# Prefills tied to work four units ahead, joined norm constants, merged output planes and column kinds in a residual block on one core

## The chip, the cores and the metric

The kernel runs on one core of one Trainium2 chip. The metric is the device time of one execution in microseconds (us), as the median of several runs. A ratio, with its 95% interval, is taken from the record: it compares one kernel's fast runs with the other kernel's fast runs of the same rounds on the same chip, so it is not quite the ratio of the medians quoted beside it.

TensorE is the matmul engine, VectorE and ScalarE work elementwise, GpSimd does small things and issues the accumulating output writes, SyncE issues most of the other transfers (DMAs). In the traces here the engines take their instructions in the order in which the built program lists them, and they wait on semaphores for each other.

## The reference, cut to what matters

```python
def reference(x, t_emb, g1, be1, w1, w_emb, g2, be2, w2):   # B=2, C=512, 64x64, bf16
    h = conv3(_silu(gn(x, g1, be1)), w1)                    # gn: 4 groups of 128 channels
    h = h + (_silu(t_emb) @ w_emb).reshape(B, C, 1, 1)
    h = conv3(_silu(gn(h, g2, be2)), w2)
    return x + h
```

## The kernel before

The two 3x3 convolutions are computed with fewer products than nine taps: VectorE forms sums and differences of rows and columns of the input (the products' inputs, per channel tile `ct`), TensorE multiplies them with transformed weights, ScalarE takes the results out of PSUM, and VectorE combines them into output planes. The work is cut into 8 chunks (layer, batch, half image) of 4 units (output channel tiles): 32 units. Units 0 to 15 are layer 1, units 16 to 31 layer 2.

The order of all instructions is not written by hand. The kernel first records about 2,800 operations with an assumed cost each, a small list scheduler in the kernel orders them, and they are then issued in that order. The scheduler knows the exact elements that an operation reads and writes. The semaphores are put in afterwards by the layer that records the program, which goes by the operands' access patterns.

The parts that the change touches:

```python
        # output planes of a unit: two instructions of 1024 elements
        tt(tw(SD, 512), M(0, 2), M(2, 2), AD, nm + "s")          # two sums into SD, SD+512
        tt(M(0, 2), M(2, 2), M(0, 2), SB_, nm + "d")             # two differences into MB
        scal(se[0], M(2), M(1), 8.0, nm + "8")
        scal(se[1], M(3), M(1), 2.0, nm + "2")
        scal(se[2], A(SD + 1024, [[1, 512]]), A(SD + 512, [[1, 512]]), 4.0, nm + "4")
        tt(yr(0), A(MB, [[0, 2], [1, 512]]), A(MB + 1024, [[512, 2], [1, 512]]), AD, nm + "y")
        tt(yr(16), A(SD, [[0, 2], [1, 512]]), A(SD + 1024, [[-512, 2], [1, 512]]), AD, nm + "y")

        # column kinds of one channel tile: four instructions
        for kind, (i, j, op) in enumerate(((32, 33, SB_), (1, 0, SB_), (33, 0, SB_), (33, 0, AD))):
            tt(A(vnest(c, ct, kind, 0), [[1, 256 * nf]]), X(i), X(j), op, nm)

    # norm constants of one channel tile: small matmuls into PSUM bank 7, a VectorE copy
    # out of it, five further small instructions, of which one on GpSimd (the -0.5 power)
    def gn_chain(layer, b, ct, mes, name, SB=7, slack=2.5): ...

                # x copied into the output in DRAM, which the result is later added to
                dma(out[b, k, ch][:, r0:r1], x[b, k, ch][:, RW + r0:RW + r1], [], [...],
                    P * YF, f"pre{c}{k}")
```

The last one is called a prefill below: 32 copies of 260 KB from DRAM to DRAM, which depend on nothing.

## Time and profile before

| | before |
|---|---|
| median | 527.14 us of 3 runs (524.67 to 527.91) |
| span of the profiled run | 523.0 us |
| TensorE / VectorE / ScalarE busy | 473.8 / 445.7 / 383.9 us |
| last matmul to the end | 14 us |

The view by stretches of time, kernel before. Columns: stretch in us, its length, busy time of TensorE (matmuls), its weight loads, VectorE, ScalarE, GpSimd, each with the number of instructions, then granted TensorE clock, share of the DMA engines, GB/s.

```profile
core 0: us, PE busy (x) PEld busy (x) DVE busy (x) ACT busy (x) POOL busy (x), PEclk, DMA share, GB/s
60.00:136.00 76.00, 53.20 (x223) 23.71 (x221) 56.22 (x124) 56.31 (x126) 1.46 (x2) 0.80 0.64 201
136.00:200.00 64.00, 61.58 (x348) 33.45 (x347) 58.46 (x151) 58.29 (x105) 1.47 (x2) 1.00 0.39 131
200.00:285.00 85.00, 79.40 (x446) 42.98 (x445) 79.72 (x178) 65.31 (x121) 7.99 (x15) 0.99 0.61 199
285.00:335.00 50.00, 50.00 (x315) 30.58 (x314) 48.55 (x102) 38.14 (x52) 2.90 (x7) 0.98 0.51 167
335.00:509.00 174.00, 174.00 (x1239) 119.82 (x1236) 154.61 (x257) 120.46 (x137) 21.04 (x25) 1.00 0.57 129
```

In the last two lines TensorE is busy for all of 50 and 174 us: layer 2, which begins at 310 us, has no hole. The holes are in the first line (76.00 - 53.20 = 22.8 us) and in the third.

From the list of waits, kernel before (who waited, for whom, us in total, times, longest):

```profile
PE psum L369 <- DVE ar L318: 21.8, 8, 6.7
...
PE psum L369 <- DVE fs L421: 8.1, 5, 5.3
```

L318 is the helper of all large VectorE additions, L421 the copy that empties bank 7 in a chain of norm constants. The longest of its waits in the timeline of the kernel before (start, length, what, in brackets the idle time before it and what ended it):

```profile
274.39 7.83 DVE L318 TENSOR_TENSOR ar<-ar 128x1024 f16<-128x1024 f16 x12
...
277.57 0.50 PE L369 MATMUL psum<-fs,ones_neg 128*128 128x2 f32 x4
277.93 1.03 PE L369 MATMUL psum<-ar 128*128 128x256 f16 x8
...
284.07 0.15 DVE L421 COPY fs<-psum 128x2 f32<-128x2 f32 x1
...
284.27 6.07 PE L369 MATMUL psum<-ar 128*128 128x512 f16 x29 [5.31 <-DVE fs L421]
```

TensorE put its four small matmuls into bank 7 at 277.57 us, and the copy that frees the bank stood in VectorE's order behind long additions until 284.07 us.

The two sizes of the large additions, from the groups by shape (busy us, mean ns of one, idle time before them), and the prefills (first and last start, us), kernel before:

```profile
L318 DVE TENSOR_TENSOR ar<-ar 128x1024 f16<-128x1024 f16 x272 | 180.4, 693 | 18.4 <-ACT ar L341 17.3
...
L318 DVE TENSOR_TENSOR ar<-ar 128x2048 f16<-128x2048 f16 x16 | 19.5, 1220 | 7.0 <-ACT ar L341 7.0
```

```profile
L354 SPq DMA_DIRECT2D out_dram<-in_x_dram x32: 511/532/647, 39.2 to 115.6; - x32
```

### The profile page before, as it was taken

The page shows a single profiled execution, that of the slowest core. Times are in us where ns is not written, and L with a number is a line of the kernel's source. Part 1 is how long each engine was busy: PE and PEld are TensorE (multiplying, and loading weights), DVE is VectorE, ACT ScalarE, POOL GpSimd, SP SyncE. Part 2 cuts the span into 40 slices and gives each one's busy share as a digit, 9 for nine tenths or more (in the row PEclk, how much of TensorE's full clock was granted, in tenths as well). Part 3 has the DMA queues.
Part 4 walks back from the last instruction along what each step waited for, and adds up shares of the span by engine and source line. Part 5 has one row for each costly group of instructions (what it writes and reads, how often), then busy time and mean ns, then how long its engine had stood idle before and what let it go on. Part 6 is the DMA issues. An engine that isn't in the chain of part 4 may idle for free.

```text
span 523.0 us, 8270 instructions
## 1 busy us (share of the span) xinstructions
PE 473.8 (91%) x2889; PEld 281.2 (54%) x2889; DVE 445.7 (85%) x932; ACT 383.9 (73%) x614; POOL 44.1 (8%) x75
## 2 busy tenths in 40 slices
PE   6999986664999999999995999999999999999990
PEld 5744332322545554555553557766666777766660
DVE  1799757588799999999999999999999999986443
ACT  4896838588999986686987678597866878665440
POOL 3100000000100001001100000120200111001000
PEclk9999989785999999999998999999999999999995
DMA  8938848674545236467575456663773776268422
GB/s 328 327 111 249 272 126 249 182 233 159 163 154 175 74 115 205 143 186 219 189 245 204 133 185 214 144 143 106 161 168 104 174 162 171 72 120 155 65 42 41
DMA packets 41065, 87.18 MB, mean 167 GB/s; under 512 B 6464, under 2 KB 16448, under 8 KB 41024
## 3 DMA queue, kind: packets, MB, share of 16 engines
q1 hardware_dynamic: 35808, 77.07, 45.0%
q0 software_dynamic: 4928, 9.59, 12.0%
q8 instruction: 22, 0.36, 0.3%
q14 instruction: 19, 0.16, 0.1%
q10 hardware_dynamic: 288, 0.01, 0.0%
HBM read 62.25 MB, written 31.85 MB: 180 GB/s over the span
## 4 chain that ended last, share of the span: by engine, by line
issue 21%; DVE 20%; PE 6%; POOL 2%; ACT 2%; POOLq 0%; DVEq 0%; ACTq 0%
DVE ar L318 19%; PE psum L369 6%; POOL out_dram L354 2%; ACT ar L341 2%; DVE ar L322 1%; POOLq L1121 0%; DVE fs L846 0%; DVE fs L422 0%; DVE fs L435 0%; POOL ar L358 0%; DVE fs L433 0%; DVE fs L421 0%; DVE fs L841 0%; POOLq L354 0%; DVE fs L425 0%
## 5 line engine op out<-in xcount | busy, mean ns | idle before, releaser
L369 PE MATMUL psum<-ar 128*128 128x256 f16 (+2 forms) x2737 | 456.1, 327 | 30.1 <-DVE ar L318 21.8
L318 DVE TENSOR_TENSOR ar<-ar 128x1040 f16<-128x1040 f16 (+6 forms) x681 | 412.2, 654 | 48.6 <-ACT ar L341 31.6
L369 PEld LDWEIGHTS <-ar 128*128 128x128 f16 (+1 forms) x2729 | 264.4, 98 | 216.0 <-issue 31.5
L341 ACT ACTIVATE ar<-ar 128x512 f16<-128x512 f16 (+7 forms) x206 | 169.7, 852 | 62.0 <-DVE ar L318 47.9
L341 ACT ACTIVATE ar<-psum 128x512 f16<-128x512 f32 (+2 forms) x221 | 154.7, 716 | 55.6 <-PE psum L369 29.8
L341 ACT ACTIVATE ar<-ar,fs 128x2112 f16<-128x2112 bf16 (+1 forms) x32 | 68.5, 2144 | 7.4 <-DMA ar<-h_scr 2.6
L354 POOL DMA_DIRECT2D out_dram<-ar x16 | 19.3, 1206 | 126.8 <-DVE ar L318 105.6
L322 DVE TENSOR_SCALAR ar<-ar 128x512 f16<-128x512 f16 (+2 forms) x72 | 26.0, 385 | 1.6 <-ACT ar L341 1.6
L428 POOL TENSOR_TENSOR fs<-fs 128x1 f32<-128x1 f32 x16 | 13.5, 847 | 159.2 <-DVE fs L425 158.9
L341 ACT ACTIVATION_READ_ACCUMULATOR ar<-psum 128x1 f32 x96 | 19.4, 202 | 0.0
L369 PE MATMUL psum<-ar,ones_bf 128*128 128x260 bf16 x64 | 10.1, 317 | 4.4 <-DMA ar<-in_x_dram 4.4
L358 POOL MEMSET ar<- 128x65 f16 (+4 forms) x27 | 4.6, 212 | 110.9 <-DVE ar L318 38.2
L369 PEld LDWEIGHTS psum<-fs,ones_neg 128*128 128x128 f32 x72 | 10.3, 206 | 2.5 <-DVE fs L958 1.6
L341 ACT ACTIVATION_READ_ACCUMULATOR ar<-ar 128x1 f32 x56 | 10.7, 191 | 0.0
L369 PE MATMUL psum<-fs,ones_neg 128*128 128x1 f32 (+1 forms) x72 | 10.0, 247 | 0.7 <-DVE fs L958 0.7
L369 PEld LDWEIGHTS <-ones_bf 128*128 128x128 bf16 x64 | 6.9, 112 | 6.2 <-issue 3.1
L354 POOL DMA_DIRECT2D ar<-ar x4 | 3.7, 922 | 73.6 <-ACT ar L341 52.2
L421 DVE COPY fs<-psum 128x2 f32<-128x2 f32 x16 | 2.5, 156 | 6.8 <-PE psum L369 6.8
L889 DVE SCALAR_TENSOR_TENSOR ar<-psum,ident 128x128 bf16<-128x128 f32 x4 | 1.2, 289 | 5.5 <-PE psum L369 5.5
L969 DVE BATCH_NORM_STATS2 fs<-ar 128x6 f32<-128x512 bf16 x8 | 5.4, 686 | 0.0
L433 DVE TENSOR_TENSOR fs<-fs 128x1 f32<-128x1 f32 x16 | 2.5, 155 | 2.4 <-POOL fs L428 2.4
L422 DVE SCALAR_TENSOR_TENSOR fs<-fs 128x1 f32<-128x1 f32 x16 | 3.4, 213 | 0.0
(43 smaller groups left out, 30.5 us busy)
## 6 DMA issues: line engine op xcount, KB each, us to landing
ar<-in_w_dram SPq DMA_DIRECT2D x32, 384.0 KB, 3.7
ar<-in_x_dram SPq DMA_DIRECT2D x16, 552.5 KB, 4.1
out_dram<-in_x_dram SPq DMA_DIRECT2D x32, 260.0 KB, 4.0
h_scr<-ar SPq DMA_DIRECT2D x16, 520.0 KB, 3.2
ar<-h_scr SPq DMA_DIRECT2D x16, 520.0 KB, 4.5
out_dram<-ar POOLq DMA_DIRECT2D x16, 520.0 KB, 6.0
u_scr<-ar SPq DMA_DIRECT2D x16, 384.0 KB, 2.9
ar<-u_scr SPq DMA_DIRECT2D x4, 1536.0 KB, 7.1
```

The source lines that it names most:

```text
L318: pl.op("DVE", 0.075 + 0.000521 * out.n, lambda: nc.vector.tensor_tensor(out=out.ap, in0=a.ap, in1=b.ap, op=op), regs(a, b), regs(out), name)
L322: pl.op("DVE", cost or 0.075 + 0.00026 * out.n, lambda: nc.vector.tensor_scalar(out=out.ap, in0=a.ap, scalar1=s, scalar2=None, op0=ALU.mul ...
L341: lambda: nc.scalar.activation(out=out.ap, in_=a.ap, func=func, scale=sc, **kw), regs(*rr), regs(*ww), name)
L354: lambda: eng.dma_start(out=out, in_=in_, **kw), regs(*r), regs(*w), name, lat=3.2 if sw else None)
L358: pl.op("POOL" if eng == "gpsimd" else "DVE", 0.08 + 0.0005 * out.n, lambda: e.memset(out.ap, v), (), regs(out), name)
L369: nc.tensor.matmul(out.ap, lhsT=lhsT.ap, rhs=rhs.ap, start=st, stop=sp, skip_group_check=True)
L421: pl.op("DVE", 0.16, lambda: nc.vector.tensor_copy(out=F(tot, 2).ap, in_=ps.ap), regs(ps), regs(F(tot, 2)), name)
L422: pl.op("DVE", 0.1, lambda: nc.vector.scalar_tensor_tensor(out=F(nv).ap, in0=F(tot).ap, scalar=F(tot).ap, in1=F(tot + 1).ap, op0=ALU.mult, ...
L428: pl.op("POOL", 0.25, lambda: nc.gpsimd.tensor_tensor(out=F(rs).ap, in0=F(nv).ap, in1=F(NEGH).ap, op=ALU.pow), regs(F(nv)), regs(F(rs)), name)
L433: pl.op("DVE", 0.1, lambda: nc.vector.tensor_mul(out=F(s).ap, in0=F(rs).ap, in1=F(g).ap), regs(F(rs)), regs(F(s)), name)
L889: pl.op("DVE", 0.3, lambda: nc.vector.scalar_tensor_tensor(out=j2.ap, in0=g.ap, scalar=1.0 / HW, in1=ident[:], op0=ALU.mult, op1=ALU.mult, ...
L969: pl.op("DVE", 0.61, lambda e=e, q=q: nc.vector.bn_stats(out=q.ap, in_=e.ap), regs(e), regs(q), nm)
```

## The change

The intent: take the prefills out of the crowded beginning; join the norm constants of four channel tiles into one chain (12 chains become 3; the four of layer 1's batch 0 stay); save 60 VectorE instructions by merging pairs (32 output planes, 28 column pairs); and bring the scheduler's costs closer to the trace. Since the scheduler sees other operations and other costs, the order of everything changes too.

The diff, cut to its core:

```diff
-    LAT = {..., "DMA": 2.1}
+    LAT = {..., "DMA": 2.4}          # DMA rate 0.31 -> 0.3; silu + 0.18; GpSimd power 0.25 -> 0.85
 # prefills
-                        P * YF, f"pre{c}{k}")
+                        P * YF * 1.4, f"pre{c}{k}", after=ufirst[max(ucnt[0] - CFG["pre"], 0)])   # pre: 4
 # column kinds 0 and 1 by one instruction
-            tt(A(s0, [[1, 256 * nf]]), X(i), X(j), op, nm)             # four of them
+        tt(A(s0[0], [[s0[1] - s0[0], 2], [1, 256 * nf]]), X2(32, 1), X2(33, 0), SB_, nm)
+        for kind, op in ((2, SB_), (3, AD)):
+            tt(A(s0[kind], [[1, 256 * nf]]), X(33), X(0), op, nm)
 # output planes by one instruction
-        tt(tw(SD, 512), M(0, 2), M(2, 2), AD, nm + "s")
+        tt(tw(SD, 1024), M(0, 2), M(2, 2), AD, nm + "s")
-        scal(se[2], A(SD + 1024, [[1, 512]]), A(SD + 512, [[1, 512]]), 4.0, nm + "4")
+        scal(se[2], A(SD + 512, [[1, 512]]), A(SD + 1024, [[1, 512]]), 4.0, nm + "4")
-        tt(yr(0), A(MB, [[0, 2], [1, 512]]), A(MB + 1024, [[512, 2], [1, 512]]), AD, nm + "y")
-        tt(yr(16), A(SD, [[0, 2], [1, 512]]), A(SD + 1024, [[-512, 2], [1, 512]]), AD, nm + "y")
+        pq = lambda a, b, st: A(a, [[b - a, 2], [st, 2], [1, 512]])
+        tt(A(ys, [[RW, 32], [33, 2], [1, 32]]), pq(MB, SD, 0), pq(MB + 1024, SD + 512, 512), AD, nm + "y")
 # norm constants: gn_chain(..., n=1) takes n tiles; layer 2 and batch 1 of layer 1 use n=4
-        later.append(lambda: gn_chain(0, 1, ct, [(me, 0, 2)], nm))
+        if ct == CT - 1:
+            later.append(lambda: gn_chain(0, 1, 0, [(ME1, 0, 2 * CT)], "st1", n=CT))
 ... (gn2 likewise, per batch and no longer per tile)
```

The merged plane: the one instruction that now makes the output planes of a unit. Their first half lies in `MB`, their second in `SD`, 29,748 elements lower in layer 1 and 27,316 in layer 2 (from the layout).

More of the change, by code (lines that the diff above doesn't have):

```diff
@@ L31 @@
     WIN = {"DMA": 0.6}
-    LAT = {"PE": 0.12, "DVE": 0.12, "ACT": 0.15, "POOL": 0.15, "DMA": 2.1}
+    LAT = {"PE": 0.12, "DVE": 0.12, "ACT": 0.15, "POOL": 0.15, "DMA": 2.4}
     def __init__(self):
@@ L45, in space, with op @@
         self._space(name, size)
-    def op(self, eng, cost, fn, r=(), w=(), name="", chain=False, lat=None, slack=0.0):
+    def op(self, eng, cost, fn, r=(), w=(), name="", chain=False, lat=None, slack=0.0, after=None):
         o = Op()
@@ L76, in op @@
             self.chain = o.i
+        if after is not None:
+            deps.add(after)
         deps.discard(-1)
@@ L198 @@
     'np': 1,
+    'pre': 4,
     'wpe': (1, 0, 0, 0),
@@ L254 @@
     ar = pool.tile([P, NA], F16, name="ar")
-    NF = 512
+    NF = 640
     fs = pool.tile([P, NF], F32, name="fs")
@@ L339, in act @@
             kw["saturate"] = False
-        pl.op("ACT", 0.1 + 0.000833 * out.n + (0.09 if acc is not None else 0.0),
+        pl.op("ACT", 0.1 + 0.000833 * out.n + (0.09 if acc is not None else 0.0) + (0.18 if bias is not None else 0.0),
               lambda: nc.scalar.activation(out=out.ap, in_=a.ap, func=func, scale=sc, **kw), regs(*rr), regs(*ww), name)
@@ L347, in scal, with dma @@
             ts(out, a, s, name)
-    def dma(out, in_, r, w, nbytes, name="", sw=False, acc=False):
-        rate = 0.15 if acc else 0.31
+    def dma(out, in_, r, w, nbytes, name="", sw=False, acc=False, after=None):
+        rate = 0.15 if acc else 0.3
         kw = {"accum_op": ALU.add, "max_dma_last_dim": 2080} if acc else {}
@@ L353, in dma @@
         pl.op("DMA", nbytes / rate * 1e-6 if nbytes > 30000 else 0.1,
-              lambda: eng.dma_start(out=out, in_=in_, **kw), regs(*r), regs(*w), name, lat=3.2 if sw else None)
+              lambda: eng.dma_start(out=out, in_=in_, **kw), regs(*r), regs(*w), name, lat=3.2 if sw else None, after=after)
     def memz(eng, out, name="", v=0.0):
@@ L386 @@
     WJ = Fc(12)
-    NEGH = Fc(1)
-    EPSC = Fc(1)
+    NEGH = Fc(CT)
+    EPSC = Fc(CT)
     def scol(layer, b, ct):
@@ L400 @@
     nc.scalar.activation(out=fs[:, WARM:WARM + 1], in_=fs[:, WARM + 1:WARM + 2], func=ACT.Silu)
-    nc.vector.memset(fs[:, NEGH:NEGH + 1], -0.5)
-    nc.vector.memset(fs[:, EPSC:EPSC + 1], EPS)
+    nc.vector.memset(fs[:, NEGH:NEGH + CT], -0.5)
+    nc.vector.memset(fs[:, EPSC:EPSC + CT], EPS)
     nc.gpsimd.tensor_tensor(out=fs[:, WARM:WARM + 1], in0=fs[:, WARM + 1:WARM + 2], in1=fs[:, NEGH:NEGH + 1], op=ALU.pow)
@@ L408, with Fs, small, gn_chain @@
     ssb = T(s_sb[:], "s_sb")
-    def gn_chain(layer, b, ct, mes, name, SB=7, slack=2.5):
-        ps = Ps(SB, 0, [[1, 2]])
+    def Fs(c, step, n):
+        return R(fs[:, c:c + (n - 1) * step + 1:step], ("F", np.arange(n) * step + c), n)
+    def small(fn, r, w, name, cost=0.125):
+        pl.op("DVE", cost, fn, regs(*r), regs(*w), name)
+    def gn_chain(layer, b, ct, mes, name, SB=7, slack=2.5, n=1):
+        V = nc.vector
+        ps = Ps(SB, 0, [[1, 2 * n]])
         lst = []
-        for i, (c, k0, n) in enumerate(mes):
-            lst.append((Ps(SB, k0, [[1, n]]), cneg, F(c, n), i == 0, False))
-        lst.append((Ps(SB, 1, [[1, 1]]), cneg, F(EPSC), False, True))
+        for i, (c, k0, m) in enumerate(mes):
+            lst.append((Ps(SB, k0, [[1, m]]), cneg, F(c, m), i == 0, False))
+        lst.append((Ps(SB, n, [[1, n]]), cneg, F(EPSC, n), False, True))
@@ L419, in gn_chain @@
         mm(lst, name, chain=False, slack=slack)
-        tot, nv, rs = Fc(2), Fc(1), Fc(1)
-        pl.op("DVE", 0.16, lambda: nc.vector.tensor_copy(out=F(tot, 2).ap, in_=ps.ap), regs(ps), regs(F(tot, 2)), name)
-        pl.op("DVE", 0.1, lambda: nc.vector.scalar_tensor_tensor(
-            out=F(nv).ap, in0=F(tot).ap, scalar=F(tot).ap, in1=F(tot + 1).ap, op0=ALU.mult, op1=ALU.add),
-            regs(F(tot, 2)), regs(F(nv)), name)
-        pl.op("DVE", 0.1, lambda: nc.vector.tensor_scalar(
-            out=F(nv).ap, in0=F(nv).ap, scalar1=-1.0, scalar2=EPS, op0=ALU.mult, op1=ALU.max),
-            regs(F(nv)), regs(F(nv)), name)
@@ L428, in gn_chain @@
-        pl.op("POOL", 0.25, lambda: nc.gpsimd.tensor_tensor(
-            out=F(rs).ap, in0=F(nv).ap, in1=F(NEGH).ap, op=ALU.pow),
-            regs(F(nv)), regs(F(rs)), name)
+        tot, nv, rs = Fc(2 * n), Fc(n), Fc(n)
         s, nb = scol(layer, b, ct), ncol(layer, b, ct)
         g = GB + 2 * CT * layer + ct
-        pl.op("DVE", 0.1, lambda: nc.vector.tensor_mul(out=F(s).ap, in0=F(rs).ap, in1=F(g).ap),
-              regs(F(rs)), regs(F(s)), name)
-        pl.op("DVE", 0.1, lambda: nc.vector.scalar_tensor_tensor(
-            out=F(nb).ap, in0=F(tot).ap, scalar=F(s).ap, in1=F(g + CT).ap, op0=ALU.mult, op1=ALU.add),
-            regs(F(tot, 2), F(s)), regs(F(nb)), name)
+        T0, T1, N, S, B = F(tot, n), F(tot + n, n), F(nv, n), F(s, n), F(nb, n)
@@ new lines, in gn_chain @@
+        pl.op("DVE", 0.16, lambda: V.tensor_copy(out=F(tot, 2 * n).ap, in_=ps.ap), regs(ps), regs(F(tot, 2 * n)), name)
+        if n == 1:
+            small(lambda: V.scalar_tensor_tensor(
+                out=N.ap, in0=T0.ap, scalar=T0.ap, in1=T1.ap, op0=ALU.mult, op1=ALU.add), [T0, T1], [N], name, 0.2)
+        else:
+            small(lambda: V.tensor_mul(out=N.ap, in0=T0.ap, in1=T0.ap), [T0], [N], name)
+            small(lambda: V.tensor_add(out=N.ap, in0=N.ap, in1=T1.ap), [N, T1], [N], name)
@@ new lines, in gn_chain @@
+        small(lambda: V.tensor_scalar(out=N.ap, in0=N.ap, scalar1=-1.0, scalar2=EPS, op0=ALU.mult, op1=ALU.max),
+              [N], [N], name)
+        pl.op("POOL", 0.85, lambda: nc.gpsimd.tensor_tensor(
+            out=F(rs, n).ap, in0=N.ap, in1=F(NEGH, n).ap, op=ALU.pow), regs(N), regs(F(rs, n)), name)
+        small(lambda: V.tensor_mul(out=S.ap, in0=F(rs, n).ap, in1=F(g, n).ap), [F(rs, n)], [S], name)
+        if n == 1:
+            small(lambda: V.scalar_tensor_tensor(
+                out=B.ap, in0=T0.ap, scalar=S.ap, in1=F(g + CT).ap, op0=ALU.mult, op1=ALU.add), [T0, S], [B], name, 0.2)
+        else:
+            small(lambda: V.tensor_mul(out=B.ap, in0=T0.ap, in1=S.ap), [T0, S], [B], name)
+            small(lambda: V.tensor_add(out=B.ap, in0=B.ap, in1=F(g + CT, n).ap), [B], [B], name)
@@ L638, in rows_b @@
         X = lambda i: A(xb + i, [[RW, 8 * nf], [1, 32]])
-        for kind, (i, j, op) in enumerate(((32, 33, SB_), (1, 0, SB_), (33, 0, SB_), (33, 0, AD))):
-            s0 = vnest(c, ct, kind, 0)
-            tt(A(s0, [[1, 256 * nf]]), X(i), X(j), op, nm)
+        X2 = lambda i, j: A(xb + i, [[j - i, 2], [RW, 8 * nf], [1, 32]])
+        s0 = [vnest(c, ct, kind, 0) for kind in range(4)]
+        tt(A(s0[0], [[s0[1] - s0[0], 2], [1, 256 * nf]]), X2(32, 1), X2(33, 0), SB_, nm)
+        for kind, op in ((2, SB_), (3, AD)):
+            tt(A(s0[kind], [[1, 256 * nf]]), X(33), X(0), op, nm)
     ucnt = [0]
+    ufirst = {}
     prs = [0]
@@ L692, in unit @@
         nm = f"u{c}{k}"
+        if opening != 1:
+            ufirst[u] = len(pl.ops)
         last = u == 31
@@ L701, in unit @@
             OO = [O0[u % 3] + PL, O0[u % 3]]
-        if l == 0 and ch == 0 and (b, k) not in SSUM:
-            SSUM[(b, k)] = (Fc(12), Fc(2))
+        if l == 0 and ch == 0 and b not in SSUM:
+            SSUM[b] = (Fc(48), Fc(2 * CT))
         acc = lambda i: None
         if l == 0:
-            cs, cq = SSUM[(b, k)]
-            acc = lambda i: F(cs + 6 * ch + i)
+            cs, cq = SSUM[b]
+            acc = lambda i: F(cs + 12 * k + 6 * ch + i)
         fid = ACT.Identity if l == 0 else ACT.Copy
@@ L801, in unit @@
         scal(se[1], M(3), M(1), 2.0, nm + "2")
-        scal(se[2], A(SD + 1024, [[1, 512]]), A(SD + 512, [[1, 512]]), 4.0, nm + "4")
-        yr = lambda r0: A(ys + r0 * RW, [[RW, 16], [33, 2], [1, 32]])
-        tt(yr(0), A(MB, [[0, 2], [1, 512]]), A(MB + 1024, [[512, 2], [1, 512]]), AD, nm + "y")
-        tt(yr(16), A(SD, [[0, 2], [1, 512]]), A(SD + 1024, [[-512, 2], [1, 512]]), AD, nm + "y")
+        scal(se[2], A(SD + 512, [[1, 512]]), A(SD + 1024, [[1, 512]]), 4.0, nm + "4")
+        pq = lambda a, b, st: A(a, [[b - a, 2], [st, 2], [1, 512]])
+        tt(A(ys, [[RW, 32], [33, 2], [1, 32]]), pq(MB, SD, 0), pq(MB + 1024, SD + 512, 512), AD, nm + "y")
         yo = A(ys, [[24 * RW, 2], [1, PL]])
@@ L815, in unit @@
             dma(h_scr[b, k, ch], yv.ap, [yv], [K("h", b, k, ch)], P * YF * 2, nm + "st")
-            act(A8(JNK, YF), yv, ACT.Square, scale=float(HW) ** -0.5, acc=F(cq + ch), name=nm + "sq")
-            if ch == 1:
-                later.append(lambda: gn2(b, k))
+            act(A8(JNK, YF), yv, ACT.Square, scale=float(HW) ** -0.5, acc=F(cq + ch * CT + k), name=nm + "sq")
+            if ch == 1 and k == CT - 1:
+                later.append(lambda: gn2(b))
         else:
@@ L823 @@
     later = []
-    def gn2(b, k):
-        cs, cq = SSUM[(b, k)]
-        m0, me, wj, ws = Fc(2), Fc(2), WJ, Fc(1)
-        nm = f"gn2_{b}{k}"
-        E = EMB + k * BB + b
-        V = nc.vector
-        pl.op("DVE", 0.12, lambda: V.scalar_tensor_tensor(
-            out=F(wj, 12).ap, in0=F(cs, 12).ap, scalar=1.0, in1=F(SUMW, 12).ap, op0=ALU.mult, op1=ALU.mult,
-            accum_out=F(m0).ap), regs(F(cs, 12)), regs(F(wj, 12), F(m0)), nm)
-        pl.op("DVE", 0.1, lambda: V.reduce_sum(out=F(m0 + 1).ap, in_=F(cq, 2).ap, axis=AX.X),
-              regs(F(cq, 2)), regs(F(m0 + 1)), nm)
-        pl.op("DVE", 0.1, lambda: V.scalar_tensor_tensor(
-            out=F(me).ap, in0=F(m0).ap, scalar=1.0 / HW, in1=F(E).ap, op0=ALU.mult, op1=ALU.add),
-            regs(F(m0), F(E)), regs(F(me)), nm)
-        pl.op("DVE", 0.1, lambda: V.scalar_tensor_tensor(
-            out=F(ws).ap, in0=F(m0).ap, scalar=1.0 / HW, in1=F(me).ap, op0=ALU.mult, op1=ALU.add),
-            regs(F(m0), F(me)), regs(F(ws)), nm)
-        pl.op("DVE", 0.1, lambda: V.scalar_tensor_tensor(
-            out=F(me + 1).ap, in0=F(ws).ap, scalar=F(E).ap, in1=F(m0 + 1).ap, op0=ALU.mult, op1=ALU.add),
-            regs(F(ws), F(E), F(m0 + 1)), regs(F(me + 1)), nm)
-        gn_chain(1, b, k, [(me, 0, 2)], nm)
-        nb, s = ncol(1, b, k), scol(1, b, k)
-        pl.op("DVE", 0.1, lambda: V.scalar_tensor_tensor(
-            out=F(nb).ap, in0=F(E).ap, scalar=F(s).ap, in1=F(nb).ap, op0=ALU.mult, op1=ALU.add),
-            regs(F(E), F(s), F(nb)), regs(F(nb)), nm)
@@ new lines, in gn2 @@
+    def gn2(b):
+        cs, cq = SSUM[b]
+        V = nc.vector
+        nm = f"gn2_{b}"
+        wj, m0, me, ws, t = Fc(48), Fc(CT), Fc(2 * CT), Fc(CT), Fc(CT)
+        E = Fs(EMB + b, BB, CT)
+        C = F(cs, 48)
+        M0, ME, MQ, W, Tt = F(m0, CT), F(me, CT), F(me + CT, CT), F(ws, CT), F(t, CT)
+        wt = fs[:, SUMW:SUMW + 12].unsqueeze(1).to_broadcast([P, CT, 12])
+        g3 = lambda c: fs[:, c:c + 48].rearrange("p (k s) -> p k s", s=12)
+        small(lambda: V.tensor_tensor(out=g3(wj), in0=g3(cs), in1=wt, op=ALU.mult), [C], [F(wj, 48)], nm)
+        small(lambda: V.reduce_sum(out=M0.ap, in_=g3(wj), axis=AX.X), [F(wj, 48)], [M0], nm)
+        small(lambda: V.tensor_add(out=MQ.ap, in0=F(cq, CT).ap, in1=F(cq + CT, CT).ap), [F(cq, 2 * CT)], [MQ], nm)
+        small(lambda: V.scalar_tensor_tensor(
+            out=ME.ap, in0=M0.ap, scalar=1.0 / HW, in1=E.ap, op0=ALU.mult, op1=ALU.add), [M0, E], [ME], nm)
+        small(lambda: V.scalar_tensor_tensor(
+            out=W.ap, in0=M0.ap, scalar=1.0 / HW, in1=ME.ap, op0=ALU.mult, op1=ALU.add), [M0, ME], [W], nm)
+        small(lambda: V.tensor_mul(out=W.ap, in0=W.ap, in1=E.ap), [W, E], [W], nm)
+        small(lambda: V.tensor_add(out=MQ.ap, in0=MQ.ap, in1=W.ap), [MQ, W], [MQ], nm)
+        gn_chain(1, b, 0, [(me, 0, 2 * CT)], nm, n=CT)
+        S, B = F(scol(1, b, 0), CT), F(ncol(1, b, 0), CT)
+        small(lambda: V.tensor_mul(out=Tt.ap, in0=E.ap, in1=S.ap), [E, S], [Tt], nm)
+        small(lambda: V.tensor_add(out=B.ap, in0=B.ap, in1=Tt.ap), [B, Tt], [B], nm)
@@ L939 @@
     prs[0] = 2
-    S1 = {}
+    ME1 = Fc(2 * CT)
     def stats1(ct):
         nm = f"st1{ct}"
-        me = Fc(2)
+        me, mq = ME1 + ct, ME1 + CT + ct
         if CFG["st1"][ct]:
@@ L957, in stats1 @@
                 accum_out=F(me).ap), regs(F(part, 6)), regs(F(wj, 6), F(me)), nm)
-            pl.op("DVE", 0.1, lambda: nc.vector.reduce_sum(out=F(me + 1).ap, in_=F(part + 6, 6).ap, axis=AX.X),
-                  regs(F(part + 6, 6)), regs(F(me + 1)), nm)
+            pl.op("DVE", 0.1, lambda: nc.vector.reduce_sum(out=F(mq).ap, in_=F(part + 6, 6).ap, axis=AX.X),
+                  regs(F(part + 6, 6)), regs(F(mq)), nm)
         else:
@@ L973, in stats1 @@
             pl.op("DVE", 0.1, lambda: nc.vector.scalar_tensor_tensor(
-                out=F(me + 1).ap, in0=F(mv).ap, scalar=F(mv).ap, in1=F(mv + 1).ap, op0=ALU.mult, op1=ALU.add),
-                regs(F(mv, 2)), regs(F(me + 1)), nm)
-        later.append(lambda: gn_chain(0, 1, ct, [(me, 0, 2)], nm))
+                out=F(mq).ap, in0=F(mv).ap, scalar=F(mv).ap, in1=F(mv + 1).ap, op0=ALU.mult, op1=ALU.add),
+                regs(F(mv, 2)), regs(F(mq)), nm)
+        if ct == CT - 1:
+            later.append(lambda: gn_chain(0, 1, 0, [(ME1, 0, 2 * CT)], "st1", n=CT))
     def emb():
```

## The prediction

> **What bounds it.** The profile's span is 523.0 us; TensorE is busy 473.8 us (91%), VectorE 445.7, ScalarE 383.9 (busy table). By stretches of time: from about 311 to 509 us TensorE is busy all the time, and output units leave every 12.36 us at the end (28672 columns, 2.3 per ns): only fewer columns would shorten that. TensorE's idle time lies elsewhere: about 23 us between 60 and 136 us (53.2 of 76 us busy, granted clock 0.80), 5.3 us at 279 us, some 3 us in 136-200, 14 us after its last matmul.
>
> In 60-136 TensorE waits for VectorE, which makes the next transformed weights; there VectorE itself waits 11 us for weight and input loads. All 32 prefills (input copied to the output in DRAM, 260 KB each) are issued from 39 to 116 us: half of the bytes then, and 0.5 us of queue time each. Small weight loads land in 3.2 us (median) then, 2.2 us in 120-200.
>
> The wait at 279 us is TensorE before bank 7, which a norm-constant chain holds until VectorE copies it (released by the copy at L421); the copy stood behind 12 long VectorE instructions. All such waits: 8.1 us, 5 times.
>
> **What changes.**
> 1. Prefills move to about 265-460 us, two per 12 us unit. Weight loads gain about 1 us each in each of about six double-buffered rounds, plus queue delays: -4 to -10 us in 60-136. In layer 2 DMA share rises from 0.57 to about 0.7; TensorE should stay full.
> 2. Norm chains: 12 (layer 2, and batch 1 of layer 1) become 3. Nine groups of 4 small fp32 matmuls go, 0.36 us each: -3 us, of which 2 in full stretches. Fewer holds of bank 7: -5 us. VectorE loses 6-7 us of small instructions.
> 3. 32 output pairs and 28 column pairs each become one instruction. The durations 693 ns (1024 elements) and 1220 ns (2048) give 0.51 ns per element plus 166 ns, of which some 90 overlap the neighbour: 0.08 us saved each, 4.6 us of VectorE in all. The Trainium skill, "VectorE: DVE Perf Modes" (perf-mode tier table), gives tensor_tensor 1224 ns for 2048 bf16 at double rate; the trace agrees with 1220, so I expect the merged forms to keep this rate. Mostly TensorE is full there, so it buys nothing. In the last unit the merged plane must wait for ScalarE's scaling: +0.2 us.
> 4. Costs in the scheduler (DMA, silu, pow) come nearer to the trace; the order changes: +-4 us.
>
> Sum: -8 (60-136), -5 (bank 7), -2 (matmuls), +1 to 2 for new small waits: -14 us on the clock, so 514 us.
>
> **What would show it.** No DRAM-to-DRAM copy before about 240 us; small weight loads there land in about 2.3 us; TensorE idle in 60-136 falls from 23 to about 14 us; waits on the bank-7 copy under 3 us; VectorE busy about 435 us; matmuls 2853 instead of 2889; unit period in layer 2 still 12.4 us, last matmul about 14 us before the end.
>
> **What would make it wrong.** The loop of 60-136 may be bound by VectorE, ScalarE and buffers, not DMA latency: then about -7 us remain. Joining batch 1's constants makes its first silu wait for all four tiles and may leave a hole near 145 us. The reshuffled order may put another long run before a copy that TensorE needs. Prefills beside the weight stream could starve layer 2.
>
> Faster by over 2%: 0.6; within 2%: 0.36; slower: 0.04. Range 503 to 524 us.

## More of the kernel before

All operands lie in one large array `ar` in SBUF, at offsets that the kernel lays out by hand:

```python
    AB = [o, o + AF]          # input tiles (loads, silu in place)
    o += 2 * AF
    YS = [o, o + YF]          # output planes of a unit, two buffers
    o += 2 * YF
    MB = o                    # four taken-out products of a unit, 4 x 512
    o += 4 * MS
    ...
    SD0 = Z + 10016           # sums of a unit, in layer 1
    SD1 = Z + 12448           # sums of a unit, in layer 2; Z lies far below AB
```

## The result, and the profile after

| | before | after |
|---|---|---|
| median | 526.2 us of 4 runs | 533.84 us of 4 runs (533.33 to 534.28) |
| ratio | | 1.0147, 95% interval 1.0121 to 1.0172 |
| span of the profiled run | 523.0 us | 532.0 us |
| TensorE / VectorE / ScalarE busy | 473.8 / 445.7 / 383.9 us | 471.6 / 439.4 / 383.7 us |
| matmul instructions | 2889 | 2853 |

The kernel became 1.5% slower. It does less work on TensorE and on VectorE, as intended, and takes longer, so the time went into waits.

The stretches, kernel after, same columns as before:

```profile
60.00:136.00 76.00, 59.44 (x256) 26.48 (x254) 56.63 (x108) 58.58 (x132) 0.00 (x0) 0.87 0.40 123
136.00:200.00 64.00, 52.26 (x281) 28.08 (x282) 56.80 (x117) 56.94 (x100) 1.45 (x1) 0.89 0.45 150
200.00:285.00 85.00, 82.77 (x460) 44.27 (x459) 75.43 (x143) 63.02 (x116) 6.23 (x12) 1.00 0.56 180
285.00:335.00 50.00, 44.78 (x267) 26.43 (x265) 49.71 (x89) 39.66 (x58) 0.59 (x5) 0.97 0.70 243
335.00:509.00 174.00, 169.37 (x1206) 116.71 (x1205) 149.38 (x215) 116.31 (x134) 20.07 (x23) 1.00 0.63 156
```

TensorE's idle time in 60-136 us fell from 22.8 to 16.6 us, but in the next stretch it rose from 2.4 to 11.7 us, and the stretches of layer 2, full before, now have holes (5.2 us in 285-335 and 4.6 us in 335-509). From the list of waits, kernel after:

```profile
PE psum L372 <- DVE ar L321: 17.4, 5, 6.7
PE psum L372 <- ACT ar L344: 9.6, 4, 4.0
PE psum L372 <- DVE fs L975: 9.4, 1, 9.4
PE psum L372 <- DVE fs L434: 5.0, 3, 2.5
```

The line of 9.6 us for ScalarE is new, all of it in layer 2 but 1 us. L975 with 9.4 us is the last step of batch 1's statistics; in the kernel before that step, L958 there, held TensorE once, for 0.7 us. The prefills did move, and the merged shape keeps its rate (kernel after, same views as before):

```profile
L357 SPq DMA_DIRECT2D out_dram<-in_x_dram x32: 517/588/1219, 258.0 to 451.3; - x32
```

```profile
L321 DVE TENSOR_TENSOR ar<-ar 128x1024 f16<-128x1024 f16 x188 | 127.7, 693 | 19.5 <-ACT ar L344 18.1
L321 DVE TENSOR_TENSOR ar<-ar 128x2048 f16<-128x2048 f16 x64 | 79.2, 1238 | 27.8 <-ACT ar L344 16.2 <-issue 4.5 <-DMA ar<-in_x_dram 4.2
```

The second line holds a clue, read to its end: the 64 instructions of 2048 elements have VectorE idle before them for 27.8 us, where the 16 of the kernel before had 7.0.

To see where the time went, I counted matmul columns in each trace (both hold all 999,424 columns of the convolutions) and noted when each unit's share had begun, in us from the first such matmul. This is an evaluation of the trace, not a view of the profile. `f_split2`, `near` and `near_late` are experiments of below.

| start of unit | before | after | f_split2 | near | near_late |
|---|---|---|---|---|---|
| 5 | 119.51 | 108.08 | 103.49 | 107.48 | 104.62 |
| 6 | 135.38 | 137.23 | 133.62 | 136.26 | 118.92 |
| 9 | 181.09 | 181.92 | 177.90 | 180.66 | 183.21 |
| 14 | 253.49 | 255.28 | 250.28 | 252.85 | 259.40 |
| 15 | 274.84 | 270.70 | 264.57 | 267.15 | 273.69 |
| 18 | 315.11 | 317.44 | 306.90 | 308.61 | 314.60 |
| 24 | 389.43 | 391.76 | 381.22 | 382.93 | 388.92 |
| 27 | 426.58 | 433.98 | 418.62 | 420.08 | 426.26 |
| end | 488.51 | 495.93 | 480.55 | 482.02 | 488.19 |

The kernel after is 11.4 us ahead at unit 5 and 1.8 us behind at unit 6. It gains 5.9 us at unit 14, where the wait of 5.3 us for bank 7 stood, and loses 6.5 us from unit 15 to 18 and 5.1 us from unit 24 to 27. Two questions follow: what are the losses in layer 2 and at the layers' boundary, and why did 11 us vanish between units 5 and 6?

### The profile page after: what moved, and what is told of

The parts are those of the page before. It is cut to its first block, busy times and chain, and to the rows that moved or that the text cites. A ratio compares the mean times of both kernels' runs of the same rounds, so it can differ in the third digit from the quotient of the medians.

```text
span 532.0 us, 8068 instructions
## 1 busy us (share of the span) xinstructions
PE 471.6 (89%) x2853; PEld 278.0 (52%) x2853; DVE 439.4 (83%) x795; ACT 383.7 (72%) x614; POOL 38.7 (7%) x66
## 5 line engine op out<-in xcount | busy, mean ns | idle before, releaser
L321 DVE TENSOR_TENSOR ar<-ar 128x1024 f16<-128x1024 f16 (+5 forms) x621 | 408.2, 703 | 68.0 <-ACT ar L344 40.4
L344 ACT ACTIVATE ar<-ar 128x384 bf16<-128x384 bf16 (+7 forms) x206 | 170.1, 856 | 66.6 <-DVE ar L321 59.2
L344 ACT ACTIVATE ar<-psum 128x512 f16<-128x512 f32 (+3 forms) x221 | 155.1, 716 | 52.7 <-PE psum L372 25.2
L344 ACT ACTIVATE ar<-ar,fs 128x2112 f16<-128x2112 bf16 (+1 forms) x32 | 68.5, 2143 | 14.3 <-DMA ar<-h_scr 4.4
L443 POOL TENSOR_TENSOR fs<-fs 128x1 f32<-128x1 f32 (+1 forms) x7 | 8.0, 1137 | 143.5 <-DVE fs L441 143.5
L372 PE MATMUL psum<-fs,ones_neg 128*128 128x1 f32 (+3 forms) x36 | 5.2, 258 | 9.5 <-DVE fs L975 9.4
L372 PE MATMUL psum<-ar,ones_bf 128*128 128x260 bf16 x64 | 8.9, 293 | 4.5 <-DMA ar<-in_x_dram 4.5
L372 PEld LDWEIGHTS psum<-fs,ones_neg 128*128 128x128 f32 x36 | 5.0, 205 | 10.6 <-DVE fs L975 9.7
L434 DVE COPY fs<-psum 128x2 f32<-128x2 f32 (+1 forms) x7 | 1.1, 159 | 4.5 <-PE psum L372 4.5
L372 PEld LDWEIGHTS psum<-ar 2*128 2x128 f32 x8 | 1.8, 323 | 5.7 <-DVE ar L321 5.7
L372 PE MATMUL psum<-ar,s_sb 128*2 128x512 bf16 x9 | 3.1, 458 | 0.0
(49 smaller groups left out, 21.4 us busy)
```

The lines of the kernel that those rows point to most:

```text
L321: pl.op("DVE", 0.075 + 0.000521 * out.n, lambda: nc.vector.tensor_tensor(out=out.ap, in0=a.ap, in1=b.ap, op=op), regs(a, b), regs(out), name)
L344: lambda: nc.scalar.activation(out=out.ap, in_=a.ap, func=func, scale=sc, **kw), regs(*rr), regs(*ww), name)
L372: nc.tensor.matmul(out.ap, lhsT=lhsT.ap, rhs=rhs.ap, start=st, stop=sp, skip_group_check=True)
L434: pl.op("DVE", 0.16, lambda: V.tensor_copy(out=F(tot, 2 * n).ap, in_=ps.ap), regs(ps), regs(F(tot, 2 * n)), name)
L443: pl.op("POOL", 0.85, lambda: nc.gpsimd.tensor_tensor(out=F(rs, n).ap, in0=N.ap, in1=F(NEGH, n).ap, op=ALU.pow), regs(N), regs(F(rs, n)), ...
```

## The experiments

Each kernel was checked for correct output; all are correct but two, which are told as such. Those made from the kernel after start from it and change only what is said. Eighteen runs gave a result. Four kernels had to be submitted a second time, since no chip ran them the first time; hence the 2 in some labels.

### First round: undo one part of the change at a time

Parts undone: the joined chain of batch 1 (a_st1_apart), the tie of the prefills (a_pre_free), the merged pairs (a_pairs_apart). And the joined chain of batch 1 moved one unit later in the program (a_st1_late).

```diff
 # a_st1_apart
-        if ct == CT - 1:
-            later.append(lambda: gn_chain(0, 1, 0, [(ME1, 0, 2 * CT)], "st1", n=CT))
+        later.append(lambda: gn_chain(0, 1, ct, [(me, 0, 2)], nm))
 # a_st1_late
+            if c == 1 and k == 1:
+                gn_chain(0, 1, 0, [(ME1, 0, 2 * CT)], "st1", n=CT)
+                prod(2, 0)                         # no longer after unit (1, 0)
 # a_pre_free
-                        P * YF * 1.4, f"pre{c}{k}", after=ufirst[...])
+                        P * YF, f"pre{c}{k}")
 # a_pairs_apart: two instructions per output plane and per column pair, as in the kernel before
```

> The kernel after, but the norm constants of batch 1 in layer 1 again as four chains, one per channel tile, each at its old place. Theory W (TensorE had run ahead; the stretch up to 147 us is set by the statistics work of VectorE, ScalarE and the DMA queue, whose last part ends near 143 us in both kernels): the wait before the last chain stays, 7 to 12 us near 130-147, and the time is within 3 us of the kernel after (533.8). Theory J (joining four chains into one made the wait of 9.4 us): the wait falls under 2 us and the time falls by 7 to 11 us, to 523-527.

> The kernel after, with the joined chain of batch 1 and the first product that needs it one unit later in program order, so that unit 5's bank-7 matmuls need not wait for it. Theory B (order in PSUM bank 7 holds TensorE): the 9.4 + 2.5 us wait vanishes and the time falls by 8 to 12 us, to 522-526. Theory W (work of the other engines bounds this stretch): the wait at 134 us vanishes but TensorE waits as much later, at the start of chunk 2 (about 190-200 us) for the products there; time within 4 us of 533.8.

> The kernel after, with the prefills untied again and at their old cost, so the scheduler puts them early. If the tie gave back TensorE time between 60 and 136 us (as the prediction said): TensorE idle there rises from 16.6 us to about 23 us. If that gain was spent again in the wait near 140 us (theory W): column progress at unit 6 is within 3 us of the kernel after, and the total within 4 us; if prefills beside layer 2's streams cost the 5 us lost after unit 24, the total falls by about 5 us.

> The kernel after, with the output planes and the two column kinds by two VectorE instructions each, as before. If merging costs layer 2 its 5 us (a plane waits for all three scalings): holes after unit 24 vanish and the time falls by 3 to 6 us. If merging is harmless: VectorE is about 4.6 us busier, and the time is within 4 us of 533.8, moved only by the new order.

| run | median us | ratio to before, 95% |
|---|---|---|
| a_st1_apart | 543.89 | 1.0317 to 1.0373 |
| a_st1_late | 536.96 | 1.0186 to 1.0239 |
| a_pre_free | 538.94 | 1.0216 to 1.0270 |
| a_pairs_apart | 518.29 | 0.9829 to 0.9887 |

Three of the four expectations missed. Only a_st1_late came out as one of its theories (W) had said: the wait near 134 us is gone, TensorE waits as much and more in 170-215 us (19.9 us in three waits for VectorE), and the time is 3.1 us longer. a_st1_apart took longer than both of its theories allow, and its 10 us of loss are not explained here. In a_pre_free, TensorE's idle time in 60-136 us was to rise to about 23 us and is 17.6 us; this returns below. Undoing the merges is worth 15 us, far more than the 3 to 6 us of the theory that blamed them; the other three made the kernel slower. But each of these kernels was scheduled anew, so its whole order differs. The next round keeps the order.

### Second round: the same order, other instructions

In f_split2 the scheduler sees the kernel after, so the order is the same to the last instruction, but where a merged instruction would be issued, two are issued, one after the other. In f_merge2 and b_merge2 the scheduler sees pairs (as a_pairs_apart and as before do), and the merged instruction is issued at the place of the second half. a_nudge2 changes one assumed cost by 0.2% and nothing else.

```diff
 # f_split2, at the place of the merged instruction
-            nc.vector.tensor_tensor(out=full[0].ap, in0=full[1].ap, in1=full[2].ap, op=op)
+            for o, (a, b) in zip(outs, ins):
+                nc.vector.tensor_tensor(out=o.ap, in0=a.ap, in1=b.ap, op=op)
 # a_nudge2
-        pl.op("DVE", 0.075 + 0.000521 * out.n, lambda: nc.vector.tensor_tensor(
+        pl.op("DVE", 0.075 + 0.000520 * out.n, lambda: nc.vector.tensor_tensor(
```

> The kernel after with its instruction order kept exactly, but each merged output plane and column pair issued as two VectorE instructions, back to back in the same place. Theory I (the merged instructions themselves cost: a plane that waits for three scalings): no gain to be had here either, as the place is the same; only 60 x 0.08 us more VectorE: 533.8 to 538. Theory O (the order that the scheduler found makes the 15 us between this and the version with pairs apart): the same, 533 to 538. Were the 2048-element form slow in itself, the time would fall below 532.

> The order of the version with pairs apart (518.3 us), kept exactly, with each pair merged into one instruction at the place of its second half. Theory O: as fast or up to 4 us faster, 514 to 519. Theory I (merging delays what waits for the first half or makes the plane wait): 3 us or more slower, over 521, up to after's 534.

> The kernel before in its own order, with only the pairs merged at the place of the second half: 60 VectorE instructions fewer. Theory O: 522 to 526.5 (TensorE is full in most places, so at most 4 us). Theory I: over 529.

> The kernel after with one number of the scheduler's cost model nudged by 0.2 per cent (0.521 to 0.520 ns per element of a VectorE tensor-tensor): the same instructions, only a new order. Theory O: the order alone moves the time by several us; any value from 518 to 545, at least 3 us from 533.8. Were orders equivalent, it would be within 1 us of 533.8.

| run | median us | ratio to before, 95% |
|---|---|---|
| f_split2 | 518.78 | 0.9852 to 0.9891 |
| f_merge2 (wrong result) | 561.27 | 1.0641 to 1.0705 |
| b_merge2 (wrong result) | 559.15 | 1.0617 to 1.0678 |
| a_nudge2 | 541.36 | 1.0283 to 1.0321 |

f_split2 contradicts both theories as I had written them: the order is that of the kernel after, and it is 15 us faster, with 60 instructions more. Nor is the merged shape slow in itself, the third possibility in that expectation, although the time did fall below 532 us: a merged plane measures 1224 ns, its two halves 686 ns each; a column pair 1284 ns, its halves 716 ns each. a_nudge2 shows that the order is worth something beside this (7.5 us for a cost changed by 0.2%), but it cannot explain f_split2. Something happens to the same instruction at the same place when it is one and not two.

f_merge2 and b_merge2 are failed experiments. By the scheduled order, in two or three of the 32 units a later operation that overwrites an input of the first half stands between the two halves (in b_merge2, for one, the taking-out of unit 11 before the plane of unit 10), so deferring the first half reads overwritten data. Their times cannot be used.

### What the merged plane waits for

The trace of the kernel after shows VectorE idle directly before planes for things that a plane has no use for. Three places in its timeline:

```profile
58.16 2.31 DVE L321 TENSOR_TENSOR ar<-ar 128x2048 f16<-128x2048 f16 x3 [1.85 <-DMA ar<-in_x_dram]
...
232.23 2.05 DVE L321 TENSOR_TENSOR ar<-ar 128x2048 f16<-128x2048 f16 x3 [2.71 <-DMA ar<-ar]
...
372.57 2.15 ACT L344 ACTIVATE ar<-ar,fs 128x2112 f16<-128x2112 f16 x1 [0.47 <-DMA ar<-h_scr]
374.62 1.00 ACT L344 ACTIVATE ar<-psum 128x1024 f16<-128x1024 f32 x1
374.81 1.23 DVE L321 TENSOR_TENSOR ar<-ar 128x2048 f16<-128x2048 f16 x1 [2.12 <-ACT ar L344]
```

At 58.16 us the plane waited for a load of the input, at 232.23 us for a transfer from one place of `ar` to another, at 374.81 us for the silu of an input tile (the 128x2112 activation). A plane reads only `MB` and `SD` and writes `YS`. Input tiles lie in `AB`, which lies between `SD` and `MB`.

The Trainium skill, "Perfetto Trace Analysis" (Identifying Dependency Chains), advises to look at the instruction's text for the semaphores it waits on. The built program's lists for the plane of unit 19, kernel after and the later version `near` (with the waits of the semaphore instructions directly before it):

```
after:  TensorTensor ar<-ar 128x32x2x32 [waits DMAHW0,DMASW5,DMAHW2,Activation,Pool]
near:   TensorTensor ar<-ar 128x32x2x32 [waits DMASW5,Activation]
```

Over the 32 planes of the kernel after there are 51 waits on hardware DMA queues and 13 on GpSimd; over the 64 half planes of f_split2 there are 12 and 0. GpSimd's writes to `ar` are zero rows of input tiles and zero columns, none of which a plane reads. In the trace, adding the idle time of VectorE directly before planes: 1.3 us in the kernel before, 19.4 us after, 3.1 us in f_split2.

So the theory: an operand whose two halves lie 27,000 to 30,000 elements apart is taken, when the semaphores are put in, for the whole span between them. Then the plane waits for whatever was last written in between (loads, silu, zero rows), and, if so, writers of those buffers wait for the plane too. The scheduler doesn't know it, since it counts exact elements.

### Third round: the same instructions in the same order, the buffer moved

In `near` the sums buffer lies directly behind `MB`, so that the merged operand spans nothing foreign. The scheduler is given the old addresses, so the order of all five engines is that of the kernel after; comparing the built programs instruction by instruction confirmed it, here and for the three other pairs below.

```diff
     MB = o
     o += 4 * MS
+    SN = o
+    o += 4 * MS
...
+        S_ = lambda i, dims: R(A(SN + i, dims).ap, A(SD + i, dims).reg, ...)   # issued at SN, scheduled as SD
-        pq = lambda a, b, st: A(a, [[b - a, 2], [st, 2], [1, 512]])
+        def pq(a, i, st):
+            at = lambda s: A(a, [[s + i - a, 2], [st, 2], [1, 512]])
+            return R(at(SN).ap, at(SD).reg, 2048)
```

near_nudge and near_pre_free are a_nudge2 and a_pre_free with the buffer near. near_old_cost gives the scheduler the old costs.

> The kernel after, same merged instructions in the same order; only the sums buffer that the merged plane reads with its second half is put directly behind the buffer of the first half, instead of 29,700 or 27,300 elements below it. In the built program the waits of the 32 merged planes fall from 51 to 12 on hardware DMA queues and from 13 to 0 on GpSimd. Theory S (the wide span of the merged operand makes the program wait for writers of buffers that lie between): 516 to 520, like the split version (518.8). Theory L (the plane must wait for all three scalings and holds both buffers longer): stays at 530 to 534.

> The nudged order (541.4 us with the distant buffer), with the buffer near. Theory S: falls by 12 to 25 us, to 516-529, and the remaining distance to the near version (both 2,675 scheduled operations, different orders) shows what an order alone is worth, 5 us at most. Theory L: stays over 537.

> The near version with the prefills untied and at their old cost. If tying them is worth what the prediction said (4 to 10 us between 60 and 136 us): 522 to 528. If TensorE's gain there is spent in the wait for the last statistics near 140 us: within 3 us of the near version.

> The near version with the scheduler's old costs (DMA latency and rate, silu, pow). If the corrected costs matter: 3 us or more slower than near. If they only reshuffle: within 3 us either way.

| run | median us | ratio to before, 95% | same order, buffer far away |
|---|---|---|---|
| near (5 rounds) | 518.69 | 0.9852 to 0.9902 | after, 533.84 |
| near_nudge | 524.47 | 0.9961 to 1.0021 | a_nudge2, 541.36 |
| near_pre_free | 517.97 | 0.9828 to 0.9896 | a_pre_free, 538.94 |
| near_old_cost | 531.40 | 1.0096 to 1.0164 | not run |

Three pairs with the same instructions in the same order differ only in where one buffer lies, by 15, 17 and 21 us. The two kernels of a pair ran in different jobs; by their ratios to the kernel before, the differences are 14, 16 and 20 us. The theory is shown in this form: the distance within one operand costs it. The place of the buffer alone does not, since f_split2 leaves it far away and is as fast as near. That the recording layer treats the operand as its whole span is inferred from the lists of waits; I did not read it from that layer. In `near`, the idle time before planes is 3.2 us. Lines of near that answer to those of after: waits of TensorE, the group of 2048 elements, and the plane of unit 19, which now starts while the silu still runs:

```profile
PE psum L374 <- DVE ar L323: 16.7, 5, 6.2
...
PE psum L374 <- DVE fs L979: 8.4, 1, 8.4
...
PE psum L374 <- DVE fs L436: 4.2, 2, 2.5
```

```profile
L323 DVE TENSOR_TENSOR ar<-ar 128x2048 f16<-128x2048 f16 x64 | 78.7, 1236 | 11.6 <-ACT ar L346 11.4
```

```profile
362.69 2.15 ACT L346 ACTIVATE ar<-ar,fs 128x2112 f16<-128x2112 f16 x1
362.88 1.21 DVE L323 TENSOR_TENSOR ar<-ar 128x2048 f16<-128x2048 f16 x1
```

The waits of TensorE for ScalarE, 9.6 us in the kernel after, are gone from near's list. Since the order is the same, moving the buffer removed them too; the chain from a plane to each of these waits was not followed step by step. `near` with 518.7 us is also as fast as f_split2 with 518.8, so once the waits are gone, merging gains nothing measurable in the total and costs nothing, though VectorE is busy for 437.1 us instead of f_split2's 440.9.

near_pre_free answers another question: with the prefills back at the beginning the time is 518.0 us, within 0.7 us. No gain from tying them is seen. But this kernel was scheduled anew, and orders alone spread over 6 us (fifth round), so some us in either direction cannot be excluded.

### Fourth round: where the rest of the expected gain went

near is 6 us faster than before; the prediction had expected 14 without knowing of the wide operand. near_late moves batch 1's chain one unit later; near_norms_apart undoes the joining of all chains; b_wide and b_near apply only the merges to the kernel before, with the sums buffer far and near.

```diff
 # near_norms_apart: gn2 and the chains of batch 1 per channel tile, as in the kernel before
 # b_wide: the kernel before with the planes and column pairs of the change, nothing else
 # b_near: b_wide with SN behind MB, as in near
```

> The near version with batch 1's joined chain and its first product one unit later. Theory W (VectorE, ScalarE and the DMA queue bound this stretch): the wait of 8.4 us near 140 us turns up again at the start of chunk 2 (unit 8 to 9), time within 3 us of near (518.7). Theory B (bank 7's order is what holds TensorE): 507 to 512.

> The near version with all twelve chains apart again (layer 2 and batch 1 of layer 1). If joining is worth the 7 us that the prediction gave it (bank-7 holds 5, matmuls 2): 523 to 528. If not: 516 to 521.

> The kernel before with only the merges (planes and column pairs), scheduled anew, the sums buffer far away as in the change: 530 to 545 if the wide operand costs here as it does in the kernel after.

> The same with the sums buffer next to its neighbour; same instructions in the same order as b_wide. Theory S: 8 to 20 us under b_wide, and within 6 us of before (525).

| run | median us | ratio to before, 95% |
|---|---|---|
| near_late | 528.54 | 1.0014 to 1.0102 |
| near_norms_apart | 529.17 | 0.9997 to 1.0095 |
| b_wide | 555.08 | 1.0519 to 1.0590 |
| b_near | 540.98 | 1.0231 to 1.0337 |

b_wide and b_near are a fourth pair with one order: the distance costs 14 us without any other part of the change. But b_near, though free of it, is still 15 us slower than before, where at most 6 were expected. Since the merges cost nothing in near, its new order is the likely reason; that was not tested.

near_late answers the question of units 5 and 6. In the kernel after the wait sits here:

```profile
143.45 0.15 DVE L975 TENSOR_REDUCE fs<-fs 128x1 f32<-128x6 f32 x1
...
143.66 1.01 PE L372 MATMUL psum<-fs,ones_neg 128*128 128x8 f32 x4 [9.45 <-DVE fs L975]
...
146.93 0.16 DVE L434 COPY fs<-psum 128x8 f32<-128x8 f32 x1
...
147.14 1.44 PE L372 MATMUL psum<-ar 128*128 128x512 f16 x3 [2.46 <-DVE fs L434]
```

The last statistics of batch 1 end at 143.6 us; in the kernel before the same step ended at 143.0 us. TensorE had run ahead and now waited for them. In near_late, where TensorE needn't, the columns are 17.3 us ahead of near at unit 6 and 2.5 us behind at unit 9. Its longest wait in 190-215 us:

```profile
PE psum L374 <- DVE ar L323: 7.3, 1, 7.3
```

So the hole moved to the first products of chunk 2. This speaks for the work of VectorE, ScalarE and the SyncE queue up to there as what bounds the stretch, and against bank 7; which of the three it is was not separated. That direction is what theory W said; its size (within 3 us) was missed, near_late is 10 us slower. near_norms_apart is 10 us slower than near as well, more than the 7 us that joining was given; by its columns it is 3.9 us behind at unit 6, before its first layer-2 chain, and 7.9 us behind at unit 9.

The runs together also tell what TensorE's idle time in 60-136 us depends on, which no single run was made for. From the view by stretches, a_st1_apart and a_pre_free:

```profile
60.00:136.00 76.00, 53.03 (x222) 24.14 (x221) 55.87 (x118) 54.39 (x121) 2.32 (x3) 0.80 0.39 124
60.00:136.00 76.00, 58.35 (x258) 25.77 (x255) 59.27 (x114) 61.59 (x139) 0.00 (x0) 0.87 0.64 199
```

| TensorE idle in 60-136 us | batch 1's chains apart | joined |
|---|---|---|
| prefills at the beginning | before 22.8 | a_pre_free 17.6, near_pre_free 18.7 |
| prefills tied | a_st1_apart 23.0, near_norms_apart 22.5 | after 16.6, near 16.9 |

The idle time goes with the joined chain and hardly with the prefills. All these orders differ, but in every kernel with a correct result it is 13 to 20 us with the chain joined (13 kernels) and 22 to 28 us with the chains apart (5 kernels). Why joining lets TensorE run ahead was not tested.

### Fifth round: what an order alone is worth

near_late, near_norms_apart and near_old_cost each had a new order, so I ran two more that differ from near in nothing else: the cost of 0.521 ns per element of near at 0.522 and at 0.519.

> The near version with the same scheduler number nudged the other way, 0.522 instead of 0.521 ns per element: same instructions, another order. With near (518.7) and near_nudge (524.5) it tells how far orders of the same work spread: anywhere from 514 to 532, most likely 518 to 526.

> The same with 0.519: 514 to 532, most likely 518 to 526. If all four orders lie within 2 us of each other but near_nudge, the spread is a fluke of one order; if they spread over 6 us or more, no part of the change worth less than that can be read from one re-scheduled run.

| assumed ns per element | 0.519 | 0.520 | 0.521 (near) | 0.522 |
|---|---|---|---|---|
| median us | 523.86 | 524.47 | 518.69 | 518.27 |

Four orders of the same instructions spread over 6 us. A part of the change worth less than that can't be read from one run that was scheduled anew. The 10 to 13 us of near_late, near_norms_apart and near_old_cost are more than these four show, but four orders are few; what joining the chains and the corrected costs are worth, apart from the order, stays open.

Six versions beat both kernels: near, near_pre_free, near_n522, f_split2 and a_pairs_apart at 518.0 to 518.8 us, 1.2 to 1.5% under before, and near_n519 by a hair (ratio 0.9963, interval 0.9944 to 0.9982).

## Why the prediction was wrong

It said 514 us, from 503 to 524; the kernel takes 533.8.

- **The step that failed most** is step 3: "so I expect the merged forms to keep this rate. Mostly TensorE is full there, so it buys nothing." The rate was right: the merged planes take 1224 ns, what the Trainium skill, "VectorE: DVE Perf Modes" (perf-mode tier table), gives for 2048 bf16 elements. But I had costed a merged instruction by its own duration alone, and looked at its inputs only for the scalings. That its operand reaches over 27,000 elements of other buffers was in the diff, and its waits cost 15 us (533.84 against 518.69, same order); VectorE's idle time directly before planes is 19.4 us against 3.2. In the sum, the term that had this wrong is "+1 to 2 for new small waits". That merging by itself buys nothing was right (near against f_split2).
- **"-8 (60-136)"** failed in its mechanism. Its first half came: small weight loads landed in 2.0 us (median between 39 and 120 us; I had said 2.3, before it was 3.2; with the prefills back it is 2.7 in a_pre_free and 3.0 in near_pre_free), which fits the Trainium skill, "DMA: Bandwidth & Descriptors" (Issuing engines are not separate DMA queues): all transfers share the same 16 engines. But TensorE's idle time does not follow the loads. It fell by 6 us in the kernel after, and with the prefills back at the beginning it stays at 17.6 and 18.7 us, while with batch 1's chains apart and the prefills tied it is 23.0 and 22.5 us. And what TensorE gained there it spent in a wait for other engines' work (9.4 us at 134-144); near and near_pre_free take 518.7 and 518.0 us. The caveat "may be bound by VectorE, ScalarE and buffers" was right. The hole near 145 us, which joining "may leave", came too, but not clearly for the reason given: with the chains apart, a_st1_apart has one wait of 9.7 us between 120 and 150 us.
- **"-5 (bank 7)"** was right in kind: the wait of 5.3 us at 279 us is gone, and near gains 7.1 us on before between units 14 and 15. The waits for the copy are 5.0 us in the kernel after and 4.2 in near, where I had said under 3. Between units 14 and 15, near takes 14.3 us, near_norms_apart 17.5 and the kernel before 21.4; how much of this is the joining and how much the order is not separated.
- **"-2 (matmuls)"**: the count is 2853, as said. The term was too small to be seen by itself.
- **VectorE busy about 435 us**: 439.4. The busy time counts an overlap of neighbours once (84 ns at the median of such pairs in the kernel before). Added up singly, VectorE's instructions take 22.2 us less in the kernel after, the busy time only 6.3 us less.
- **"unit period in layer 2 still 12.4 us"**: wrong in the kernel after (5.1 us lost between units 24 and 27), right in near from unit 18 on; its unit 17 takes 14.7 us.
- **"+-4 us" for the order** was too small: four orders of near spread over 6 us, and the change of one cost by 0.2% moved the kernel after by 7.5 us. Other re-scheduled versions were 10 to 13 us slower than near, but with other parts changed as well.

## What to carry to other kernels

Before two instructions are merged, look at where the halves of each operand lie: if foreign buffers lie between, compare the lists of waits of the built program before and after, and place the halves side by side, which was worth 14 to 21 us here. When one part of a scheduled kernel is to be judged, keep the order fixed (issue other instructions at the same places, or move an address while the scheduler sees the old one); otherwise the order's own spread, 6 us here, hides the part. And time that one engine gains ahead of a wait for others is not yet time gained: ask what the next wait is bound by.

## What the Trainium skill lacked or had wrong

- No page says that an operand with two distant halves can be synchronised as if it covered all between (inferred here from the lists of waits). Measured: 51 against 12 waits on hardware DMA queues over 32 planes, 13 against 0 on GpSimd, and 14 to 21 us. "Perfetto Trace Analysis" (Identifying Dependency Chains) gives the way to find it, but not this cause.
- "VectorE: DVE Perf Modes" (perf-mode tier table) has one figure for a tensor_tensor of 2048 16-bit elements, 1224 ns. The planes agree (1224 ns), but a column pair, which reads runs of 32 elements from both inputs, takes 1284 ns at the same size; halves with that pattern take 715 ns, the other forms of 1024 elements 683 to 689 ns (kernel before).
